# One core, cosine attention into a leaky-relu MLP: every operation issued from one written list

## The chip, the cores and the metric

One core of a Trainium2 chip runs the kernel. The metric is the time of one execution in device microseconds; the kernel before was timed three times, and its median is 416.56 us (415.56 to 416.66). Five engines work side by side, each through its own instructions in order: TensorE (PE; its weight loads are shown as PEld), VectorE (DVE), ScalarE (ACT), GpSimd (POOL) and SyncE (SP). SP and POOL also issue the DMAs, each in the order of its own queue; ACT issues three at the very start.

## The reference, cut

```python
def _attn_ref(q, k, v, tau):          # 8 x 12 x 448 x 64 each, tau = 0.1
    q_n = q / (np.linalg.norm(q, axis=-1, keepdims=True) + 1e-06)
    k_n = k / (np.linalg.norm(k, axis=-1, keepdims=True) + 1e-06)
    scores = np.matmul(q_n, k_n.transpose(0, 1, 3, 2)) / tau
    scores = scores - np.max(scores, axis=-1, keepdims=True)
    attn = np.exp(scores)
    attn = attn / (np.sum(attn, axis=-1, keepdims=True) + 1e-09)
    return np.matmul(attn, v)

def _moe_ref(x, w_in, w_out):         # 3584 x 768, 768 x 2048, 2048 x 768
    h = x @ w_in
    g = np.maximum(0.01 * h, h)
    return g @ w_out
```

The heads of a batch are put side by side between the two (x has 8 x 448 rows and 12 x 64 columns). All inputs and the output are float32; the kernel multiplies in bf16.

## The kernel before

**Slots.** The 96 heads are worked off as 48 slots of q and k, each some 448 KB. Slots 0 to 11 (batches 0 and 1) hold one pair of heads each, q and k together; slots 12 to 47 come in twos, q of two pairs of heads in the even one and k in the odd one, and two such slots are a *unit*. A slot passes through: load (`load_qk`, on SP; slots 0 to 5 are loaded ahead of everything), squares on POOL (L226, L218), sums of the squares on DVE (`sums`, L240, L234), square roots on ACT (`roots`: a logarithm and an exponential, L247 and L248), and `normalise` on DVE (reduce and reciprocal, L255 and L256, and the multiply that writes the bf16 tile qn, L272, L262). Slots 0 to 11 are then transposed on PE against an identity (L286) and copied out of PSUM by DVE (L327); the others are transposed on DVE (L308) and laid out as qkT by six DMAs of SP for each unit (L317).

**Attention.** A score tile is 128 keys by two heads of 448 queries and takes two banks of PSUM: `scores` for slots 0 to 11 (L348; three tiles for a slot, and a fourth for the keys that remain of two slots), `quad_tiles` (L419, seven tiles for a unit) after that. ACT takes the exponential of each into a bf16 tile pe (L357, L425). The sums over the keys and the products with v run on 32-column strips of PE (L368 for the first six j, a j being four heads; L444 for the ten groups of units). ACT turns the sums into reciprocals (L379 and L380, L453 and L456), and DVE multiplies the products by them into xT (L399, L469, L475), the transposed input of the MLP.

**MLP.** It goes by eight chunks c, one for a batch (384 or 512 columns). `first(c, m)` makes one of 16 tiles of the hidden layer: six matmuls with w_in (L496), then a leaky relu on ACT into hT (L507). `second(c, ts, half)` makes 128 rows by 384 columns of the output: 16 matmuls with w_out (L533), a copy by DVE (L543), and a store by SP (L550) when the row is whole. For chunk 0 the tiles of `first` can be done in parts, so many of the six matmuls at a time.

**Loads on POOL's queue.** v in pieces (`load_v`, L178, one for each of the first six j; `load_v_rem`, L186, what remains of them; `load_vq`, L204, one for each group), w_in in four parts of 768 KB (`load_w_in`, L104) and w_out in three: the first half of its columns whole (1536 KB), and the second half in two parts, rows 0 to 7 and 8 to 15 of its 16 blocks (`load_w_out`, L110).

**Holds.** Two helpers only make a queue wait. `hold` lets POOL copy one element of a slot's qn (L618), and what POOL issues after it waits until that slot is normalised. `hold_loads(s)` does the same to SP's queue with a DMA of one element of qn of slot s into the tile `behind` (L615).

**Banks.** `banks(count)` deals the eight banks of PSUM to the matmuls, always the ones dealt longest ago, unless one is kept. While `deals["apart"]` holds, that is in the loop over the first six slots, pairs come from banks 0 to 3 and single ones from 4 to 7.

**What sets the order.** Slots 0 to 5 run in a loop (L654 to L736), slots 6 to 11 in a stretch written out by hand (L747 to L863), and the rest in visits of three quad tiles each (L868 to L963), into which whole tiles of `first` and `second` are dealt by their cost. Between them stand *fills*: matmuls on constant data (L607), 20 at the start and then in threes and twos, 37 in all. In the loop the sums of a later slot stand around the norm of the next one:

```python
        if n and s > 1:
            sums(n, (0,))
        if not last:
            normalise(s + 1)
        ...
        elif s in (2, 3):
            hold_loads(s + 1)
            load_qk(s + 6)
```

and in the stretch by hand, with s = 6, stand `load_v(s // 2 + 1)`, `load_w_out(1, 0, MT // 2)`, later `load_w_out(1, MT // 2)`, `load_v(s // 2 + 2)`, and the holds and loads `hold_loads(s + 3)`, `load_qk(s + 6)`, `hold_loads(s + 4)`, `load_qk(s + 7)`, `hold_loads(s + 5)`, `load_qk(s + 8)`, `load_qk(s + 9)`.

**Buffers.** Four for loaded slots, three each for qn, squares and norms, six for qkT, 25 for pe, three for v of the first six j, two for v of the groups, one for hT, three for output rows.

Of the kernel before, what the change touches and what calls it, by code (L numbers as in the profile page):

```python
# [12 lines left out]
AX = mybir.AxisListType  # L13


@with_exitstack
def kernel(
# [25 lines left out]
    WARM = 20  # L43
    NEWQ = 2 * NQ
    PER = 3
# [25 lines left out]
    age = [0] * 8  # L71
    kept = {}
    deals = {"n": 0, "apart": True, "width": 128}

    def banks(count, keep=None):
        lo, hi = (0, 8) if not deals["apart"] else (0, 4) if count == 2 else (4, 8)
        x = min(
            (i for i in range(lo, hi, count) if not set(range(i, i + count)) & set(kept.values())),
            key=lambda i: max(age[i : i + count]),
        )  # L80
        deals["n"] += 1
        age[x : x + count] = [deals["n"]] * count
        if keep:
            kept[keep] = x
        return ps[:, x] if count == 1 else ps[:, x : x + count]

    def given_back(keep):
        deals["n"] += 1
        age[kept.pop(keep)] = deals["n"]

# [115 lines left out]
    def squares(s, eng=gp, parts=(0, 1)):  # L211
        if s >= NSLOT:
            return
        sq = sqt[s % 3]
        if s >= OLD:
            sqs[s] = sq
            x = raw[s].rearrange("p (t d) -> p t d", d=D)
            gp.tensor_tensor(sq[:, :, :D], x, x, op=ALU.mult)  # L218
            return
        sqs[s] = halves(sq.rearrange("p t d -> p (t d)"), D + 1)  # L220
        for i in parts:
            x, y = raw[s][i], sqs[s][i]
            if eng is nc.scalar:
                nc.scalar.activation(y[..., :D], x, func=AF.Square)
            else:
                eng.tensor_tensor(y[..., :D], x, x, op=ALU.mult)  # L226

    def sums(s, parts=(0, 1)):
        if s >= NSLOT:
            return  # L230
        if s not in ss:
            ss[s] = smp.tile([128, 14], F32, name="ss")
        if s >= OLD:
            nc.vector.tensor_reduce(  # L234
                ss[s], sqs[s], axis=AX.X, op=ALU.add
            )
            return
        for i in parts:
            o = ss[s][:, 0:8] if i == 0 else ss[s][:, 8:14]
            nc.vector.tensor_reduce(  # L240
                o.rearrange("p (h t) -> p h t", h=2), sqs[s][i], axis=AX.X, op=ALU.add
            )

    def roots(s):
        if s >= NSLOT:
            return
        nc.scalar.activation(ss[s], ss[s], func=AF.Ln)  # L247
        nc.scalar.activation(norms[s % 3][:, :, 0], ss[s], func=AF.Exp, scale=0.5)  # L248
# [3 lines left out]
    def normalise(s):  # L252
        if s >= NSLOT:
            return
# [29 lines left out]
    def one(tp, s, lo, hi):  # L284
# [10 lines left out]
    def transposed():  # L295
        return banks(1).bitcast(BF16)[:, : 7 * 128].rearrange("p (t c) -> p t c", c=128)
# [3 lines left out]
    def transposes(s):  # L300
        if s >= NSLOT:
            return
        if s >= OLD:
            u, which = divmod(s - OLD, 2)
            if which == 0:
                turned[u] = ttp.tile([128, 2, 2, S], BF16, name="tt")
            to = turned[u][:, :, which].bitcast(F32)
            nc.vector.transpose(  # L308
                out=to.rearrange(("p g (c m) -> p m g c", "p g (m c) -> p m g c")[which], m=7),
                in_=qn[s].bitcast(F32).rearrange("p m (g c) e -> p m g (c e)", g=2),  # L310
            )
            if which == 0:
                return
            for w, pair in enumerate(UNITS[u][1]):
                dst = qtp.tile([128, 2, S], BF16, name="qkT")
                for r0, of, n, g in ((0, 0, 32, 0), (32, 0, 64, 1), (96, 32, 32, 0)):
                    nc.sync.dma_start(  # L317
                        out=dst[r0 : r0 + n],
                        in_=turned[u][64 * w + of : 64 * w + of + n, g],
                    )  # L320
                qkT[pair] = dst.rearrange("p t c -> p (t c)")
            return
        dst = qtp.tile([128, 7, 128], BF16, name="qkT")
        qkT[s] = dst.rearrange("p t c -> p (t c)")
        tp = transposed()
        one(tp, s, 0, 7)
        nc.vector.tensor_copy(out=dst, in_=tp)  # L327
# [6 lines left out]
    def scores(s, kis):  # L334
        key_tiles([(s, ki) for ki in kis])

    def key_tiles(which):

        tiles = []
        for s, ki in which:  # L340
            sc = banks(2)
            tiles.append(sc)
            width = deals["width"] if ki < 3 else min(deals["width"], 64)
            for p in range(0, 128, width):
                x, c0 = (qkT[s - 1 + p // 64], 448 + p % 64) if ki == 3 else (qkT[s], 512 + 128 * ki + p)
                for a in range(2):
                    rows = slice(64 * a, 64 * a + 64)
                    nc.tensor.matmul(  # L348
                        out=sc[p : p + width, a, :S], lhsT=x[rows, c0 : c0 + width],
                        rhs=x[rows, 0:S], start=True, stop=True,  # L350
                    )
        for (s, ki), sc in zip(which, tiles):
            if ki == 3:
                dst = pr[s // 2] = pe_tile()
            else:
                dst = pe[s, ki] = pe_tile()
            nc.scalar.activation(out=dst, in_=sc[:, :, :S], func=AF.Exp, scale=inv_tau)  # L357
# [17 lines left out]
    def totals(j):  # L375
        sm = banks(1)
        strip_products(j, sm, lambda g, ki: ones, lambda g: ones_rem[:, g // 2])
        rb = rbp.tile([128, 2, S], F32, name="rb")[:, 0]
        nc.scalar.activation(rb, sm[:, :S], func=AF.Ln)  # L379
        nc.scalar.activation(rb, rb, func=AF.Exp, scale=-1.0)  # L380
        rbs[j] = rb

    pos = {}

    def products(j, e, po=None):
        b, jj = divmod(j, NQ)
        if po is None:
            po = banks(1, (j, e))
        pos[j, e] = po
        vm = vb[j].rearrange("p h t (d e) -> p h t e d", e=2)  # L390
        vr = vrb[b % 2].rearrange("p j g (d e) -> p j g e d", e=2)
        strip_products(j, po, lambda g, ki: vm[:, g, ki, e], lambda g: vr[:, jj, g, e])

    def scale(j, e):
        b, jj = divmod(j, NQ)
        m, half = divmod(b, 2)
        if m not in xT:
            xT[m] = xtp.tile([128, KT, 2 * S], BF16, name="xT")
        nc.vector.tensor_tensor(  # L399
            xT[m][:, 2 * jj + e, half * S : (half + 1) * S], pos.pop((j, e))[:, :S], rbs[j],  # L400
            op=ALU.mult,
        )
        if (j, e) in kept:
            given_back((j, e))
# [3 lines left out]
    def quad_tiles(which):  # L408

        tiles = []  # L410
        for u, i in which:
            sc = banks(2)
            tiles.append(sc)
            for strip in range(4):
                x = qkT[UNITS[u][1][strip // 2]]
                c0 = S + 64 * i + 32 * (strip % 2)
                for a in range(2):
                    rows = slice(64 * a, 64 * a + 64)
                    nc.tensor.matmul(  # L419
                        out=sc[32 * strip : 32 * strip + 32, a, :S], lhsT=x[rows, c0 : c0 + 32],  # L420
                        rhs=x[rows, 0:S], start=True, stop=True,
                    )
        for (u, i), sc in zip(which, tiles):
            pq[u, i] = pe_tile()
            nc.scalar.activation(out=pq[u, i], in_=sc[:, :, :S], func=AF.Exp, scale=inv_tau)  # L425
# [3 lines left out]
    def group_products(g, e):  # L429


        us = [u for u, (gg, _) in enumerate(UNITS) if gg == g]
        two = len(us) == 2
        po = banks(2)
# [14 lines left out]
        return po  # L449

    def group_logs(g, po):
        grb[g] = rbp.tile([128, 2, S], F32, name="rb")
        nc.scalar.activation(grb[g], po[:, :, :S], func=AF.Ln)  # L453
# [10 lines left out]
    def group_scale(g, e, po):  # L464
        js = GROUPS[g]
        for w in range(2):
# [6 lines left out]
            for n in range(2):  # L473
# [4 lines left out]
                )  # L478

# [7 lines left out]
    def first(c, m, kts=range(KT)):  # L487
        c0, n = chunk_cols(c)
        if c not in hT:
            hT[c] = htp.tile([128, MT, 512], BF16, name="hT")  # L490
        if (c, m) in begun:
            pm, done = begun.pop((c, m))
        else:
            pm, done = banks(1, (c, m, "begun") if len(kts) < KT else None), 0
# [7 lines left out]
        if done + len(kts) < KT:  # L502
            begun[c, m] = pm, done + len(kts)
            return
        if (c, m, "begun") in kept:
            given_back((c, m, "begun"))
        nc.scalar.activation(out=hT[c][:, m, :n], in_=pm[:, :n], func=AF.Prelu, alpha=0.01)  # L507

# [16 lines left out]
    def second(c, ts, half):  # L525
# [472 lines left out]
```

## Time and profile before

| what | value |
|---|---|
| median of three runs | 416.56 us |
| the profiled execution: its time, its span | 416.8 us, 415.0 us |
| PE from its last matmul to the end of the span | 2.9 us |
| score tile, exponential of it | 0.19 us of PE, 0.84 us of ACT |
| six w_in matmuls of 384, of 512 columns | 0.98 us, 1.30 us |
| 16 w_out matmuls | 2.60 us |
| square, sum, norm of a late slot | 1.69 (POOL), 1.05 and 1.6 us (DVE) |
| landing of a late slot's q, k | 4.1, 4.6 us after the issue |

The span runs from the first to the last instruction; the execution's own time is 1.8 us longer. In the profile a line number is that of the kernel before; "idle before" is how long the engine stood still ahead of a group, with what ended it. Landing is counted from the issue of a DMA to the arrival of its last byte.

### The profile page before, as it was taken

Reading aid. Unit: us, or ns where it says so; the run is one execution under the profiler, and the core shown is the slowest. Engines: PE = TensorE matmul, PEld = TensorE weight load, DVE = VectorE, ACT = ScalarE, POOL = GpSimd, SP = SyncE. Lnnn points to the kernel's source line nnn. Section 1 sums busy time; section 2 is a strip of 40 time slices with the busy share of each in tenths; the row PEclk is TensorE's granted clock in tenths of the full one; section 3 lists DMA queues with packets and bytes.
Section 4 is the critical chain, followed back from the end, with each engine's and each line's share of the span. In section 5 each row is a group of like instructions: output and inputs, shape, how many; then the busy total and the mean of one; then the engine's idle time right before and its main releaser. Section 6 shows DMA issues by size and latency. Waiting matters only on the chain.

```text
span 415.0 us, 11326 instructions
## 1 busy us (share of the span) xinstructions
PE 405.8 (98%) x4783; PEld 212.2 (51%) x4799; DVE 221.4 (53%) x387; ACT 250.5 (60%) x431; POOL 115.1 (28%) x150
## 2 busy tenths in 40 slices
PE   8799999999999999999999999999999999999997
PEld 3235555544555555544455555554445555654465
DVE  5878879756778556766484964464621301210021
ACT  4997877378657785667865688547764464004300
POOL 4885556133234132413331433122210000000000
PEclk9999999999999999999999999999999999999999
DMA  7999998965377851884285681742442100020022
GB/s 184 233 208 222 216 232 176 258 178 127 57 208 184 206 127 24 206 230 97 51 190 153 149 235 44 173 128 84 91 90 66 53 39 3 38 77 0 2 76 76
DMA packets 41980, 53.82 MB, mean 130 GB/s; under 512 B 12490, under 2 KB 32330, under 8 KB 41930
## 3 DMA queue, kind: packets, MB, share of 16 engines
q1 hardware_dynamic: 25738, 41.01, 35.1%
q0 software_dynamic: 15504, 11.80, 19.8%
q8 instruction: 37, 0.61, 0.6%
q10 hardware_dynamic: 688, 0.30, 0.2%
q14 instruction: 13, 0.11, 0.1%
HBM read 45.61 MB, written 11.01 MB: 136 GB/s over the span
## 4 chain that ended last, share of the span: by engine, by line
PE 93%; DMA 2%; ACT 1%; POOL 1%; SPq 1%; issue 1%; DVE 0%; POOLq 0%
PE ps L533 36%; PE ps L496 36%; PE ps L444 9%; PE ps L419 7%; PE ps L368 3%; PE ps L348 2%; DMA xT<-in_k_dram 1%; DMA xT<-in_q_dram 1%; ACT pe L357 1%; POOL sq L226 1%; PE ps L286 1%; SPq L133 0%; DVE qn L272 0%; POOL v_rem L186 0%; SPq L141 0%
## 5 line engine op out<-in xcount | busy, mean ns | idle before, releaser
L533 PE MATMUL ps<-w_out_sb,hT 128*128 128x384 bf16 (+1 forms) x912 | 151.3, 323 | 0.0
L496 PE MATMUL ps<-xT,w_in_sb 128*128 128x384 bf16 (+1 forms) x754 | 150.1, 352 | 0.8 <-issue 0.2
L425 ACT ACTIVATE pe<-ps 128x896 bf16<-128x896 f32 x126 | 108.9, 916 | 47.1 <-PE ps L419 47.1
L533 PEld LDWEIGHTS <-hT 128*128 128x128 bf16 x912 | 86.5, 98 | 64.0 <-issue 10.3
L496 PEld LDWEIGHTS <-w_in_sb 128*128 128x128 bf16 x768 | 72.6, 98 | 74.3 <-issue 9.8
L507 ACT ACTIVATE hT<-ps 128x384 bf16<-128x384 f32 (+1 forms) x128 | 67.4, 553 | 56.1 <-PE ps L496 54.9
L543 DVE COPY osb<-ps 128x384 f32<-128x384 f32 (+1 forms) x57 | 31.2, 547 | 101.4 <-PE ps L533 101.3
L218 POOL TENSOR_TENSOR sq<-qk_h 128x896 f32<-128x896 f32 x36 | 60.9, 1691 | 13.0 <-DMA qk_h<-in_k_dram 8.5
L618 POOL CAST seen<-qn 128x1 f32<-128x1 bf16 x46 | 8.5, 185 | 166.3 <-DVE qn L262 156.5
L262 DVE TENSOR_TENSOR qn<-qk_h,r 128x896 bf16<-128x896 f32 x36 | 43.3, 1203 | 1.2
L234 DVE TENSOR_REDUCE ss<-sq 128x14 f32<-128x910 f32 x36 | 37.9, 1053 | 1.1 <-POOL sq L218 1.1
L357 ACT ACTIVATE pe<-ps 128x896 bf16<-128x896 f32 x42 | 36.0, 918 | 2.4 <-PE ps L348 2.3
L419 PE MATMUL ps<-qkT 64*32 64x448 bf16 x1008 | 36.5, 353 | 0.0
L255 DVE TENSOR_REDUCE r<-norms 128x14 f32<-128x28 f32 x48 | 8.6, 178 | 48.7 <-ACT norms L248 48.1
L469 DVE TENSOR_TENSOR xT<-ps,rb 128x448 bf16<-128x448 f32 x32 | 18.4, 615 | 23.2 <-PE ps L444 21.5
L308 DVE STREAM_TRANSPOSE tt<-qn 128x448 f32<-128x448 f32 x36 | 29.6, 821 | 0.9
L444 PE MATMUL ps<-pe,vq 64*32 64x448 bf16 x1008 | 27.0, 349 | 0.0
L247 ACT ACTIVATE ss<-ss 128x14 f32<-128x14 f32 x48 | 10.3, 215 | 23.6 <-DVE ss L234 23.1
L419 PEld LDWEIGHTS <-qkT 64*32 64x32 bf16 x1008 | 13.0, 91 | 19.2 <-issue 14.2
L444 PEld LDWEIGHTS <-vq 64*32 64x32 bf16 x1008 | 14.5, 92 | 8.0 <-issue 0.3
L444 PE MATMUL ps<-pe,ones 64*32 64x448 bf16 x560 | 15.1, 349 | 0.0
L348 PE MATMUL ps<-qkT 64*64 64x448 bf16 (+1 forms) x132 | 12.8, 359 | 2.1 <-ACT pe L357 1.2
(53 smaller groups left out, 218.1 us busy)
## 6 DMA issues: line engine op xcount, KB each, us to landing
qk_h<-in_q_dram SPq DMA_DIRECT2D x36, 224.0 KB, 4.1
qk_h<-in_k_dram SPq DMA_DIRECT2D x36, 224.0 KB, 4.6
out_dram<-osb SPq DMA_DIRECT2D x20, 384.0 KB, 2.3
qkT<-tt SPq DMA_DIRECT2D x72, 56.0 KB, 3.2
qkT<-tt SPq DMA_DIRECT2D x36, 112.0 KB, 3.4
vq<-in_v_dram POOLq DMA_DIRECT2D x16, 224.0 KB, 4.7
w_in_sb<-in_moe_w_in_dram POOLq DMA_DIRECT2D x4, 768.0 KB, 10.4
out_dram<-osb SPq DMA_DIRECT2D x15, 192.0 KB, 3.7
```

The costliest lines, as they stand in the source:

```text
L218: gp.tensor_tensor(sq[:, :, :D], x, x, op=ALU.mult)
L234: nc.vector.tensor_reduce(ss[s], sqs[s], axis=AX.X, op=ALU.add)
L262: nc.vector.tensor_tensor(qn[s].rearrange("p m d e -> p m e d"), raw[s].rearrange(f"p ({t[1:-1]} d) -> p m e d", e=n, d=D), r.rearrange(f" ...
L308: nc.vector.transpose(out=to.rearrange(("p g (c m) -> p m g c", "p g (m c) -> p m g c")[which], m=7), in_=qn[s].bitcast(F32).rearrange("p ...
L357: nc.scalar.activation(out=dst, in_=sc[:, :, :S], func=AF.Exp, scale=inv_tau)
L419: nc.tensor.matmul(out=sc[32 * strip : 32 * strip + 32, a, :S], lhsT=x[rows, c0 : c0 + 32], rhs=x[rows, 0:S], start=True, stop=True,)
L425: nc.scalar.activation(out=pq[u, i], in_=sc[:, :, :S], func=AF.Exp, scale=inv_tau)
L444: nc.tensor.matmul(out=po[32 * strip : 32 * strip + 32, w, :S], lhsT=weights, rhs=pq[us[x if two else 0], i][rows, a, :], start=(i == 0), ...
L496: nc.tensor.matmul(out=pm[:, :n], lhsT=w_in_sb[:, kt, m * 128 : (m + 1) * 128], rhs=xT[c // 2][:, kt, c0 : c0 + n], start=(done + i == 0), ...
L507: nc.scalar.activation(out=hT[c][:, m, :n], in_=pm[:, :n], func=AF.Prelu, alpha=0.01)
L533: nc.tensor.matmul(out=po2[:, : hi - lo], lhsT=hT[c][:, m, ts * 128 : (ts + 1) * 128], rhs=w_out_sb[:, m, half * HALF + lo : half * HALF + ...
L543: nc.vector.tensor_copy(out=o[:, cols], in_=po2[:, : hi - lo])
```

## The change

All operations are now issued by one loop over a written list, `ORDER`. Each entry is a name and its numbers, looked up in a table of functions. What belonged together in one helper is taken apart, so that each engine's part has an entry of its own: a matmul group and what reads it from PSUM are two steps (`k` and `x`, `q` and `y`, `f` and `r`, `s` and `o`). Banks are taken by the matmul's step under its name and given back by the reader's step; the one dealt is the one given back longest ago. The entry `tg` ends the time in which pairs and single banks come from apart halves; it stands ahead of the first score tile.

The names that the text uses: `lq` load a slot, `sq su ro no` its squares, sums, roots and norm (for slots below 12 in two parts, `.0` and `.1`), `tp tc` transposes and their copy, `tt td` transpose on DVE and the six layout DMAs, `k x` score tile and exponential of slots 0 to 11, `q y` the same for a unit, `to ln in` totals and their reciprocals of a j, `pr sc` product and scaling, `g gl gi gx` the same of a group, `f r` a tile of `first` (with the matmuls meant, if not all six) and its relu, `s o` a tile of `second` and its copy and store, `lv lr lg wi wo` the loads on POOL, `hp` and `hs` the holds of POOL and SP, `w` fills. So `f.0.3.0.1.2.3` is chunk 0, tile 3, matmuls 0 to 3.

```diff
+ORDER = """
+lq.6 qf.0.0.3 qf.1.0.3 uf.0.0.3 w.20 qf.0.3.4 sq.2.0 uf.1.0.3 sq.2.1 uf.0.3.4 lr.0.2.4 w.2 ro.0 no.0 sa.1.0
+sa.1.1 tp.0.4.7 tp.0.0.4 w.3 w.2 ta.0.0.4 su.1.1 su.1.0 tc.0.4.7 lr.0.0.2 su.2.1 ro.1 no.1 hr k.0.1 sq.3.1 tg
+lv.0 k.0.0 su.2.0 w.2 w.2 x.0.1 k.0.2 tp.1 x.0.0 x.0.2 sq.3.0 tc.1 k.1.2 ro.2 k.1.0 lq.7 k.1.1 su.3.1 x.1.2
+no.2 w.2 x.1.0 w.2 k.1.3 tp.2 su.3.0 tc.2 w.2 w.2 x.1.1 k.2.1 sq.4.1 wi.0 hp.1 hp.0 k.2.0 ro.3 x.1.3 no.3
+x.2.1 x.2.0 to.0 ln.0 sq.4.0 hp.2 lv.1 sq.5.1 k.2.2 tp.3 su.4.0 su.4.1 tc.3 k.3.2 k.3.1 pr.0.0 ro.4 sq.5.0
+x.2.2 su.5.1 wi.1 in.0 k.3.0 hp.3 x.3.2 x.3.0 sq.6.1 lv.2 sq.7.0 sq.6.0 no.4 tp.4 su.5.0 sc.0.0 tc.4 k.3.3
...
+lq.8 sc.1.0 su.6.0 wi.2 x.4.1 k.5.0 k.5.1 x.5.1 wi.3 sq.7.1 pr.1.1 sc.1.1 sq.8.0 f.0.1.0.2 k.5.3 k.5.2 x.5.0
+x.5.2 x.5.3 ro.6 f.0.3.0.1.2.3 f.0.0.0.2 f.0.0.1 sq.8.1 wo.0 hs.3 lq.9 f.0.1.3 f.0.2.0.1.2.3 su.8.0 to.2 ln.2
...
+f.0.13 ro.9 x.7.0 no.8 f.0.10 f.0.11 x.7.3 tp.8 lq.11 sq.10.1 no.9 k.6.1 k.7.2 r.0.10 tc.8 f.0.7 sq.11.0
+wo.1.0.8 hp.8 sq.11.1 x.7.2 r.0.13 x.6.1 f.0.8 tp.9 f.0.12 su.10.0 su.10.1 r.0.7 r.0.11 tc.9 f.0.14 r.0.8
+ro.10 r.0.12 k.8.2 r.0.14 x.8.2 no.10 su.11.0 k.8.1 k.8.0 to.3 tp.10 f.0.15 tc.10 su.11.1 x.8.0 x.8.1 ln.3
+r.0.15 f.0.9 k.9.1 k.9.0 ro.11 lq.13 hs.10 lq.12 hs.9 no.11 in.3 r.0.9 k.9.2 x.9.2 s.0.0.0.384 x.9.1 x.9.0
+tp.11 hs.11 o.0.0.0.384 pr.3.0 sq.12 lv.4 wo.1.8 pr.3.1 tc.11 k.10.0 sc.3.0 sc.3.1 su.12 k.10.1 k.9.3 hp.10
+sq.13 lq.15 su.13 s.0.1.0.384 x.10.1 sq.15 x.9.3 ro.12 x.10.0 no.12 k.11.0 k.11.1 k.11.2 x.11.0 tt.12 x.11.2
+s.0.2.0.384 k.10.2 lq.14 ro.13 x.11.1 x.10.2 k.11.3 x.11.3 pr.4.1 no.13 o.0.1.0.384 tt.13 su.15 to.4 to.5 lv.5
+hp.12 hp.13 hp.11 sq.14 pr.4.0 td.0 lq.17 ln.5 ln.4 in.5 ro.15 in.4 no.15 sc.4.0 o.0.2.0.384 su.14
...
+y.1.2 r.1.9 gl.0 r.1.14 r.1.15 q.1.5 q.1.6 no.20 hp.16 hp.18 g.0.0 no.19 lq.21 lq.23 r.1.13 y.1.5 q.2.0 hp.20
+sq.23 s.1.0.0.384 lq.22 gi.0 y.1.6 s.1.1.0.384 y.2.0 q.2.1 gx.0.0 o.1.0.0.384 tt.19 su.23 sq.21 hp.19 q.2.3
+sq.22 su.22 su.21 q.2.2 y.2.2 o.1.1.0.384 tt.20 y.2.1 ro.23 y.2.3 ro.21 s.1.0.384.768 lq.25 td.3 o.1.0.384.768
+q.2.6 q.2.5 q.2.4 s.1.2.0.384 s.1.1.384.768 y.2.4 y.2.5 ro.22 y.2.6 q.3.1 q.3.0 no.23 no.21 lq.24 o.1.2.0.384
...
+"""
...
-    def banks(count, keep=None):
+    age, taken = [0] * 8, {}
+    deals = {"n": 0, "apart": True}
+
+    def take(name, count):
         lo, hi = (0, 8) if not deals["apart"] else (0, 4) if count == 2 else (4, 8)
+        busy = {b for x, n in taken.values() for b in range(x, x + n)}
         x = min(
-            (i for i in range(lo, hi, count) if not set(range(i, i + count)) & set(kept.values())),
+            (i for i in range(lo, hi, count) if not busy & set(range(i, i + count))),
             key=lambda i: max(age[i : i + count]),
         )
+        taken[name] = x, count
+        return ps[:, x] if count == 1 else ps[:, x : x + count]
...
+    def give(name):
+        x, count = taken.pop(name)
         deals["n"] += 1
         age[x : x + count] = [deals["n"]] * count
...
+    for step in ORDER.split():
+        name, *args = step.split(".")
+        steps[name](*map(int, args))
```

## The prediction

> **What bounds the kernel now.** First the page's busy shares and its 40 slices.
>
> ```profile
> span 415.0 us, 11326 instructions
> ...
> PE 405.8 (98%) x4783; PEld 212.2 (51%) x4799; DVE 221.4 (53%) x387; ACT 250.5 (60%) x431; POOL 115.1 (28%) x150
> ...
> PE   8799999999999999999999999999999999999997
> ...
> DMA  7999998965377851884285681742442100020022
> ```
>
> PE is the bound: 9.2 us idle in all. Of these the windows by stage put about 5.4 us before 32 us (1.7 us until the first fill, then gaps of 0.2 to 1.4), 0.8 us between 80 and 390, and 2.9 us after the last matmul. So an order can win little, and it loses whatever PE waits. The DMA row is full up to slice 7 (72 us); that matters below. The chain of waits, asked for 12 to 34 us, shows the one large gap of the head:
>
> ```profile
> 17.59 1.00 POOL sq L226
> ...
> 18.62 0.03 DVE ss L240
> ...
> 19.23 0.18 DVE r L255
> ...
> 19.71 1.17 DVE qn L272 x2
> ...
> 20.92 0.34 PE ps L286 x3
> ```
>
> The fourth norm (`no.3`, L255) stands behind a fifth sum (`su.4.0`, L240), which waits for POOL's square; PE sat idle 1.35 us before the transposes. From about 33 us PE is never short of work. Next the queues behind the loads: the timelines of SP and POOL between 45 and 70 us, and from the DMA view the landings.
>
> ```profile
> 49.23 0.63 SPq L615 DMA_DIRECT2D behind<-qn  x1
> 49.96 1.14 SPq L152 DMA_DIRECT2D qk_h<-in_q_dram  x2
> 54.51 0.60 SPq L615 DMA_DIRECT2D behind<-qn  x1
> 55.20 1.11 SPq L152 DMA_DIRECT2D qk_h<-in_k_dram  x2
> 59.09 0.60 SPq L615 DMA_DIRECT2D behind<-qn  x1
> ```
>
> ```profile
> 48.13 0.82 POOL L178 DMA_DIRECT2D v_b<-in_v_dram  x1
> 48.95 0.90 POOL L110 DMA_DIRECT2D w_out_sb<-in_moe_w_out_dram  x1
> ...
> 54.60 0.94 POOL L110 DMA_DIRECT2D w_out_sb<-in_moe_w_out_dram  x1
> 55.55 0.76 POOL L178 DMA_DIRECT2D v_b<-in_v_dram  x1
> ...
> 57.90 1.68 POOL L218 TENSOR_TENSOR sq<-qk_h 128x896 f32<-128x896 f32 x1
> ```
>
> ```profile
> w_out_sb<-in_moe_w_out_dram POOLq DMA_DIRECT2D x2, 768.0 KB, 14.6
> ...
> v_b<-in_v_dram POOLq DMA_DIRECT2D x6, 192.0 KB, 9.2
> ```
>
> The three `behind` DMAs are `hs.9`, `hs.10`, `hs.11`. Slot 10's norm ends at 52.56 (timeline of DVE), yet `hs.10` goes out at 54.51, 5.28 us after `hs.9`; `hs.11` follows 4.58 us later, `hs.4` in the head 4.88 us after `hs.3`. All write one element of one tile; I read it so that each waits until the one before has landed: holds in a row cost about 4.9 us each. `lv.4` goes out at 48.13 and lands at 57.2 (9.1 us); the second part of the second half of w_out (`wo.1.8`) goes out at 54.60 and lands at 69.7; PE reads it from 72.1 on. Landings on POOL's queue come in order of issue: `lv.3`, issued 3.6 us after `wo.0`, took 19.9 us and landed 1.0 us after it.
>
> **The change, part by part.** Counted name by name, old driver and list hold the same 1,250 steps, the same parts of `first` and the same 37 fills; only order and deal of banks differ. Work added: 0 on every engine. I lay the durations of the rows end to end along both lists, with PE without a gap from `to.2` (33.4 us) on, and ask at each step how late what it needs would be.
>
> *Switches of PE.* Three tiles of L419 after 128-row work take 0.69 us, two after a product 0.38, so entering costs 0.69 - 3 x 0.19 = 0.12; 16 matmuls of L533 take 2.71 after strips, 2.60 after L496, so leaving costs 0.11. From `to.2` on, the old order goes in 53 times, the new one 52; from `q.0.0` on both 43 times. Worth **-0.2 us**.
>
> *The head.* Two more fills (2 x 0.215) stand before the first transposes, so the first exp (10.37) comes about 0.5 us later. `no.3` no longer waits for the fifth sum and comes about 1.3 us sooner. Between 10.4 and 33.7 us ACT idles about 2 us in all, so its 21 exps and what lies between set the pace; summed along the new list the last (`x.5.3`) ends 0.2 us sooner. Before `to.2` PE now does 14 w_in matmuls instead of 8: 6 x 0.163 = 1.0 us. Together **-1.2 us**. Bounds: -3.5 (every gap but the first closed) to +0.9: `wi.1` goes out behind both squares of slot 5, some 1.5 us later than 20.12, and lands after 10.0 us at 31.6 or later, where the third part of `first` wants it at 31.4. `lq.8`, now ahead of `hs.3`, adds 448 KB to that stretch, but takes it from the next.
>
> *Banks up to 55 us.* With all eight dealt, `k.7.0`, `k.7.2`, `f.0.7` take banks whose reader (a relu or exp) ends 0.5 us late by the sums: **+0.5** (0 to 0.8).
>
> *SP between 45 and 65 us.* Old: `hs.9 lq.12 hs.10 lq.13 hs.11 lq.14 lq.15`. New: `lq.13 hs.10 lq.12 hs.9 hs.11 lq.15 lq.14`. `lq.13` wins 9 us; `lq.12` now stands behind the hold of slot 10. Norm of 10 ends at about 52.4, `hs.10` 52.4, `lq.12` 53.1, its second DMA 53.8; landing 6.4 us (this load before), so 60.2 (4.1, its kind's median, to 7.2: 57.9 to 61.0). `hs.9` then waits until 57.3, `hs.11` until 62.2: `lq.15` goes out at 62.9 instead of 61.1, `lq.14` at 64.2 instead of 59.8.
>
> *POOL.* Old: `lv.4 wo.1.0.8 hp.10 sq.11 wo.1.8 lv.5 hp.11 sq.12`. New: `sq.11.0 wo.1.0.8 hp.8 sq.11.1 sq.12 lv.4 wo.1.8 hp.10 sq.13 sq.15 lv.5`. So `lv.4`, `wo.1.8` and `lv.5` now queue behind squares that wait for loads. `sq.12` 60.2 to 61.9, `lv.4` out at 61.9; landing between 6.0 (fastest v_b row) and 9.1: 67.9 to 71.0; with `sq.12` at its earliest 65.6, with the slowest near row, 15.3 us, 77.2. I take 69.5, as `wo.1.0.8` ahead of it (out about 50.4, 14.1 us) is through by 64.5. PE wants it for `pr.4.1`, now in front of `to.4`: from `to.2` 82 w_in matmuls (13.3), 3 x 16 of L533 (7.8), 21 score tiles (3.9), six groups of transposes (2.3), six of strips (4.5) and switches (2.0), end at 67.2, with the 0.5 above 67.7. In the old order it lands 11.5 us before its product starts (68.72); that cover is gone: **+1.8 us** (0 to +9.5). Behind it on PE stand both totals, and `wo.1.8` is next: out at 62.7, 10.4 us (w_in's four of the same size: 7.7 to 12.0; its own row 15.1), 73.1; PE gets to row 8 of it at 69.5 + 3.1 + 1.3 = 73.9. `lv.5`, behind `sq.15`, out at 71.5, lands at 77.5 to 80.6; wanted at 77.9. Together **+0.5** (0 to +4).
>
> *From 80 us on.* Loads, turns and visits are shuffled by up to 22 places, and room is given up: between 90 and 125 the sums bring readers 0.5 to 1.6 us late at some fifteen places, where the old order has none. The worst: `lq.23` out at 106.1 lands at 110.8; `sq.23 sq.21 hp.19 sq.22` (3 x 1.69 + 0.19) until 116.1; `su.22 su.21` until 118.2; only then DVE copies `o.1.1.0` out of the bank that PE wants for `s.1.2.0` at 116.4. A PE that is already 2 us late hides part. **+1.0** (0 to +3). The other lates, up to 1.1 near 207, lie within that slip. The shuffled tiles of `first` and their relus cost nothing while a relu (0.46 to 0.6) fits under the next tile (1.0 to 1.3); from 240 us on nothing is late by over 0.15. The tail is as before: last piece, copy, 96 KB store.
>
> Sum: -0.2 - 1.2 + 0.5 + 1.8 + 0.5 + 1.0 = +2.4 on the span of 415.0: 417.4. Around it lie 1.8 us (run of 416.8), and that run is 0.24 above the median of 416.56: **419.0 us**.
>
> **Rivals.** That the list is not what it says is none: `no.3` does stand ahead of `su.4.0`, and all eight banks are dealt from before `k.0.1` on. *A, faster: the loads come in time.* The place is `pr.4.1` at 67.2, the price lv.4's landing; it decides if that is before about 67.5. For it: with `lv.4`, `wo.1.8` and `lq.13` gone from 53 to 60 us, the queues hold only `wo.1.0.8` and `lq.12`, so 4.1 and 6.0 us may be the right rows. Against it: no v_b row before 60 us but two is under 9. Then -0.2 - 1.2, and the tight places cost 0.3 or win as much: 416.56 - 1.4 to -2.0, about **414.8**. *B, even.* `lv.4` costs 1, the rest 0.5: **416.6**. *C, the order is tight throughout.* If loads take 5.2 us and turns 6.9 (q and k, and tt, in the busier stretches) instead of 4.4 and 5.9, the lates between 90 and 170 grow to 3 or 4 us, and with `lv.4` at 71.0 the slip is 5 to 6: **421.5**. For it: by the sums 10 steps of PE find something more than 0.2 us late in the old order, 33 in the new. *D, PE falls to half rate.* The first fills run at 0.43 us each, the later ones at 0.215, although the granted clock is shown as 1.00; a wait of 3.5 us at `pr.4.1` might bring that back, 13 fills' time (5.6 us) at half rate, +2.8: **424**. The Trainium skill, "TensorE: Matmul & The Clock Gate", Part 1, says that PE's clock halves after an idle window of some 3.4 us and returns after as much work. No run here has such a gap; by that rule D follows from any wait that long, by the granted clock of the trace it would not.
>
> **How the numbers follow.** Forecast 0.38, A 0.27, B 0.15, C 0.13, D 0.07. A measurement of this kernel tells 0.3% (1.25 us) from no change. Slower: 0.38 + 0.13 + 0.07 = 0.58; same 0.15; faster 0.27. The forecast's own range is 417.9 to 420.8. For 8 in 10 the range goes down to 414.0 (most of A) and up to 422.5 (C, not D).
>
> **What would show it.** Right: on SP three `behind` DMAs with 4.5 to 5 us between, `lq.15` and `lq.14` after 62; `lv.4` issued after 59 behind L218; PE idle 1 us or more before the first product of j = 4, named as waiting for v_b. The gap at 19 us gone, `to.2` at 33.4 with 14 w_in matmuls before it. Wrong: no PE gap between 60 and 80 us (A), or gaps elsewhere that sum to more (C). The head is wrong if PE waits for w_in at 31 us. The forecast falls if PE's busy time changes by more than 1 us, since the work is the same.

## The result, and the profile after

The changed kernel takes **429.52 us** (median of six runs, 426.16 to 431.55), the kernel before 416.51 us beside it: a ratio of 1.0304, 95% interval 1.0257 to 1.0352. The forecast was 419.0 us: slower, as foreseen, but by 13 us instead of 2.5. The profiled execution took 429.4 us, its span is 427.4 us. In every ratio here an execution counts only if it is within 1.5% of the fastest of its kernel, which leaves out one each of e2, e7 and e13 below. Line numbers are now those of the kernel that ran: in the experiments the same line stands up to six lines higher, as the list has another length.

The page after, its first lines:

```profile
span 427.4 us, 11306 instructions
...
PE 407.8 (95%) x4782; PEld 213.8 (50%) x4799; DVE 225.4 (53%) x387; ACT 245.4 (57%) x431; POOL 122.0 (29%) x150
```

PE's work is the same, yet it now covers 95% of the span. Of the 12.4 us that the span grew, 10 are idle time of PE ahead of its last matmul (16.3 us now, 6.3 before), 2.0 are busy time, and 0.4 are the tail (3.3 us behind the last matmul, 2.9 before). The view of PE's waits names the idle time (who waits, for whom, us in total, times, longest):

```profile
PE ps L374 <- DVE qn L359: 2.7, 4, 0.9
PE ps L427 <- DVE qkT L390: 2.1, 3, 1.1
PE ps L568 <- ACT hT L582: 2.1, 2, 1.7
...
PE ps L492 <- ACT hT L582: 1.2, 1, 1.2
...
PE ps L450 <- DMA v_b<-in_v_dram: 0.2, 1, 0.2
```

The first two lines are the head (up to 29 us). The wait for v_b on which the forecast put most is 0.2 us. The relus (hT) that PE waits for are ACT's, 3.3 us of them, and exps take another 2.9; ACT is 57% busy, so it is not slow, it stands behind something. Three places show behind what.

**The head.** The chain of waits, 9 to 29 us, runs over DVE almost alone; two of its five norms (L359, two instructions each; start and time in us):

```profile
14.77 2.32 DVE qn L359 x2
...
18.77 1.16 DVE qn L359 x2
```

Before, most norms of this shape took 1.2 us. The fourth (18.77) is no longer waited for; those of slots 1, 2, 4 and 5 now take 0.5 to 1.0 us longer than they did (slot 1 1.72 at 11.05, slot 4 2.08 at 22.40, slot 5 2.16 at 26.54). POOL's timeline has what runs beside that of slot 2:

```profile
14.38 2.29 POOL L306 TENSOR_TENSOR sq<-xT 128x512 f32<-128x512 f32 x2
...
17.43 0.44 POOL L677 CAST seen<-qn 128x1 f32<-128x1 bf16 x2
```

Two squares, which take 2.29 us here and 1.82 where no norm runs, and only behind them the holds (`seen`, L677) of slots 1 and 0, which before stood ahead of the squares. Beside the norm of slot 1 POOL squares nothing; it issues four loads of v (9.97 to 12.63 us). What lengthened that norm is not shown: in the kernel before, the one at 19.71 kept its 1.16 us beside two loads. `to.2` starts at 34.56 us, 1.19 later than before; 1.0 of that are the six more w_in matmuls that now stand ahead of it, so by this trace the head lost 0.2 us. Other executions of the same head lost more (e5 and e9, below).

**80 to 98 us.** Timelines of SP, POOL, ACT and PE (start, us, instruction, in brackets the idle time before it and what ended it):

```profile
80.32 1.35 SPq L628 DMA_DIRECT2D out_dram<-osb  x2
81.78 4.67 SPq L230 DMA_DIRECT2D qk_h<-in_q_dram  x6
...
89.78 3.32 POOL L300 TENSOR_TENSOR sq<-qk_h 128x896 f32<-128x896 f32 x2 [13.94 <-DMA qk_h<-in_q_dram]
...
94.27 0.21 ACT L336 ACTIVATE ss<-ss 128x14 f32<-128x14 f32 x1 [7.01 <-DVE ss L316]
...
94.64 0.58 ACT L582 ACTIVATE hT<-ps 128x512 bf16<-128x512 f32 x1
...
95.27 1.46 PE L568 MATMUL ps<-xT,w_in_sb 128*128 128x512 bf16 x6 [1.74 <-ACT hT L582]
```

Read it upward: PE waits 1.74 us for a relu; the relu stands on ACT behind a root (L336), which has waited 7.01 us for its sum; the square on POOL has waited 13.94 us for a load. It is slot 16's: on SP it stands behind that of slot 20, and both behind the store of a finished row that waits for PE and DVE (80.32). Before, it went out at 74.31, ahead of the stores.

**217 us.** The same chain again (load, square, sum, root, relu), and then something more. Windows of 3.4 us (busy time of PE, weight loads, DVE, ACT and POOL with counts, granted clock of PE, DMA):

```profile
216.90:220.30 3.40, 1.78 (x37) 0.71 (x21) 2.46 (x5) 3.37 (x8) 3.34 (x6) 1.00 0.63 95
220.30:223.70 3.40, 3.40 (x12) 1.63 (x11) 0.00 (x0) 0.92 (x2) 0.47 (x2) 0.50 0.92 211
```

PE idles 1.62 us of one window, and in the next its clock is 0.50: 3.41 us of work at half speed, 1.7 us lost, which is nearly all of the 2.0 us of added busy time. The six runs sort by it, roughly: the one at a mean clock of 1.00 took 426.2 us, those at 0.996 (one such window) 426.6 and 429.4, those at 0.992 (two) 429.7 to 431.6.

### The profile page after: what moved, and what is told of

Its sections match the earlier page's. It is cut to its first block, busy times and chain, and to the rows that moved or that the text cites. A ratio compares the mean times of both kernels' runs of the same rounds, so it can differ in the third digit from the quotient of the medians.

```text
span 427.4 us, 11306 instructions
## 1 busy us (share of the span) xinstructions
PE 407.8 (95%) x4782; PEld 213.8 (50%) x4799; DVE 225.4 (53%) x387; ACT 245.4 (57%) x431; POOL 122.0 (29%) x150
## 4 chain that ended last, share of the span: by engine, by line
PE 68%; DVE 13%; DMA 7%; POOL 3%; SPq 3%; issue 3%; ACT 2%; DVEq 0%; POOLq 0%; ACTq 0%
PE ps L604 27%; PE ps L568 27%; PE ps L518 8%; PE ps L492 5%; DMA qk_h<-in_q_dram 4%; DVE qn L359 3%; POOL sq L300 3%; DVE ss L316 2%; DVE ss L319 1%; DVE qn L349 1%; SPq L230 1%; DMA qk_h<-in_k_dram 1%; DVE xT L550 1%; PE ps L450 1%; DVE tt L400 1%
## 5 line engine op out<-in xcount | busy, mean ns | idle before, releaser
L604 PE MATMUL ps<-w_out_sb,hT 128*128 128x384 bf16 (+1 forms) x912 | 153.3, 326 | 1.1 <-DVE osb L620 0.6
L568 PEld LDWEIGHTS <-w_in_sb 128*128 128x128 bf16 x768 | 73.4, 98 | 77.9 <-issue 12.7
L300 POOL TENSOR_TENSOR sq<-qk_h 128x896 f32<-128x896 f32 x36 | 62.3, 1737 | 140.5 <-DMA qk_h<-in_q_dram 74.1
L582 ACT ACTIVATE hT<-ps 128x384 bf16<-128x384 f32 (+1 forms) x128 | 64.0, 548 | 66.1 <-PE ps L568 35.1
L620 DVE COPY osb<-ps 128x384 f32<-128x384 f32 (+1 forms) x57 | 29.9, 543 | 99.1 <-PE ps L604 96.9
L349 DVE TENSOR_TENSOR qn<-qk_h,r 128x896 bf16<-128x896 f32 x36 | 47.8, 1328 | 2.8 <-DVE r L343 0.9
L400 DVE STREAM_TRANSPOSE tt<-qn 128x448 f32<-128x448 f32 x36 | 28.6, 810 | 6.0 <-DMA qkT<-tt 5.8
L336 ACT ACTIVATE ss<-ss 128x14 f32<-128x14 f32 x48 | 10.3, 216 | 30.9 <-DVE ss L316 28.3
L677 POOL CAST seen<-qn 128x1 f32<-128x1 bf16 x46 | 12.5, 273 | 24.9 <-DVE qn L349 20.1
L282 POOL DMA_DIRECT2D vq<-in_v_dram x20 | 12.6, 635 | 13.5 <-PE ps L518 12.7
```

Of the source, the lines that this page charges most:

```text
L349: nc.vector.tensor_tensor(qn[s].rearrange("p m d e -> p m e d"), raw[s].rearrange(f"p ({t[1:-1]} d) -> p m e d", e=n, d=D), r.rearrange(f" ...
L400: nc.vector.transpose(out=to.rearrange(("p g (c m) -> p m g c", "p g (m c) -> p m g c")[which], m=7), in_=qn[s].bitcast(F32).rearrange("p ...
L568: nc.tensor.matmul(out=pm[:, :n], lhsT=w_in_sb[:, kt, m * 128 : (m + 1) * 128], rhs=xT[c // 2][:, kt, c0 : c0 + n], start=(done + i == 0), ...
L604: nc.tensor.matmul(out=po2[:, : hi - lo], lhsT=hT[c][:, m, ts * 128 : (ts + 1) * 128], rhs=w_out_sb[:, m, lo:hi], start=(m == 0), stop=(m ...
L620: nc.vector.tensor_copy(out=o[:, lo:hi], in_=bank(("s", c, ts, lo))[:, : hi - lo])
```

## The experiments

Each is the changed kernel, or the old order issued from the list, with one stretch or queue altered; "old order" is that of each engine in the kernel before. One thing goes along with it in some runs. Banks are dealt by the order of the whole list, and where the engines' sequences were joined to a new list, the deal is another one, though PE's order is kept: against the changed kernel, 334 of 413 deals are other in e6, e7 and e14, the same 334 in all three, and 292 in e10; against e1, 214 in e8 and 108 in e12. In e4, e5, e9, e13 and e15 the deal is the changed kernel's; e2, e3 and e11, which join two orders, have deals of their own. e8 and e12 also have five loads of SP ahead of a store, as the kernel before does, where e1 has them behind it. What the runs with another deal are worth holds this too. "Over before" is the ratio less one, times 416.5 us, against the kernel before on the same chip (the changed kernel: 12.7 us).

| run | altered | ratio to before, 95% | over before |
|---|---|---|---|
| e1 | old order from the list | 1.0010 [0.9996, 1.0024] | 0.4 |
| e2 | new, old head | 1.0064 [1.0041, 1.0088] | 2.7 |
| e3 | old, new head | 1.0114 [1.0062, 1.0165] | 4.7 |
| e4 | new, slot 16 loaded first | 1.0246 [1.0210, 1.0282] | 10.2 |
| e5 | new, w_in sooner | 1.0293 [1.0268, 1.0319] | 12.2 |
| e6 | new, POOL and DVE old in the head | 1.0220 [1.0205, 1.0235] | 9.2 |
| e7 | new, queues old at 45 to 70 us | 1.0221 [1.0154, 1.0288] | 9.2 |
| e8 | e1, norm 3 ahead | 1.0026 [1.0017, 1.0036] | 1.1 |
| e9 | new, late slots in turn | 1.0133 [1.0108, 1.0159] | 5.5 |
| e10 | e6, e7 and e9 together | 1.0086 [1.0070, 1.0102] | 3.6 |
| e11 | old to 104 us, then new | 1.0166 [1.0151, 1.0182] | 6.9 |
| e12 | e1, holds behind squares | 1.0056 [1.0038, 1.0073] | 2.3 |
| e13 | new, square of slot 35 later | 1.0320 [1.0234, 1.0405] | 13.3 |
| e14 | e6 and e7 together | 1.0170 [1.0152, 1.0188] | 7.1 |
| e15 | new, loads of 36 and 37 exchanged | 1.0210 [1.0187, 1.0232] | 8.7 |
| e16 | before, norm 3 ahead | 0.9997 [0.9987, 1.0007] | -0.1 |

### Which stretch: e1 to e4 and e11

e1 issues every engine's old sequence from a list, by which the banks are dealt; e2 and e3 join one order up to `to.2` to the other one after it. In these three a few stores of finished rows stand at other places among SP's loads than in the order they come from; in e2 that puts the loads of slots 20 and 16 ahead of one store, so it holds part of e4 as well.

> Every engine and both queues in the order of the kernel before, issued from the list, banks given back by the readers and dealt from all eight from the first score tile on. Theory Q (the loss is in the order of loads and squares on the queues) and theory V (it is in the order of visits on PE and ACT) both: 416.0 to 417.5 us, PE idle 9 to 10 us. If the dealing of banks or the list itself costs: over 418.5.

> Old order up to the totals of j = 2 on every engine, new order after it. Theory H (the head lost because squares run over norms): to.2 back at 33.4 with 8 matmuls of first before it, so 0.3 us won against the changed kernel by the trace, 428.5 to 429.5 us, and the norms of slots 1 to 5 back at 1.2 to 1.3 us each (now 1.7 to 2.3). If the head were the cause of more (a late load that is felt later): 427 or less.

> New order up to the totals of j = 2, old order after it. If the loss lies behind the head (Q and V): 416.5 to 418. If what the head leaves late is felt later: over 419.

e1 is within 0.4 us of before: the list, and the banks that it deals, cost nothing that matters; the loss comes with the new order and the deal that follows from it. e2 and e3 both came out on the second side of what was expected: what the head leaves late is felt later. It is worth 4.7 us on the old rest, and the changed kernel with the old head loses 2.7 instead of 12.7. So behind an old head the late order, which e2 keeps but for slots 20 and 16 and some stores, costs 2.7 us at most; the prices below are those of one place in one kernel, not sums to be added. In e3 the one run at full clock took 418.1 us, the three with half-rate windows 422.1 to 423.1; a window costs 1.7 us, so two of them lost more than the clock explains, and they have no trace.

e4 moves two loads:

```diff
-td.0 lq.17 ... o.0.1.384.768 ... lq.20 lq.16 ... lq.18
+td.0 lq.17 lq.16 ... o.0.1.384.768 ... lq.18 lq.20
```

> The changed kernel with only the load of slot 16 moved ahead of the three copies and stores of chunk 0, and that of slot 20 behind that of slot 18. Theory Q: slot 16 issued at about 75 instead of 84.6, its square 7 us or more sooner, the PE gaps of 1.7 and 0.3 at 93 to 97 us gone and some of what follows with them: 425 to 427.5 us. Theory V: the relus stay late, gaps at 93 to 97 stay over 1.5 us, 429 to 430.

The load went out at 80.1 us, not 75 (SP was still at slot 17's), but that was enough. PE's timeline in e4:

```profile
85.41 12.91 PE L563 MATMUL ps<-xT,w_in_sb 128*128 128x512 bf16 x57
```

57 matmuls of `first` without a gap, where the changed kernel has two; 2.5 us won for two entries of 1,250, within what theory Q said, at its weak end. The gap is settled by the trace, the 2.5 us less so, as the two intervals overlap.

e11 asks the other way round: old order up to `g.0`, new after it.

> Old order on every engine up to the sums of group 0 (about 104 us), new order after it. By the gaps after 104 us in the changed kernel (0.7 at 123, 1.4 at 153, 1.6 at 217, small ones 0.5): 419.5 to 421.5. If these are only echoes of what came before: 417 to 418.5.

It lost 6.9 us, more than both answers. In its trace PE has no gap between 110 and 180 us, so those at 123 and 153 come from what stands ahead of 104 us (or from the deal of banks, which is another one here too); 1.1 us stand at the seam (103 us), and 2.2 at 212 to 233, so the one at 217 does not. Of the 6.9 us 3.3 are idle time of PE ahead of its last matmul, 0.4 the tail, and 3.2 busy time at full clock (409.0 us, 405.8 before). About 1 us of that is no work: the trace of before lacks 16 matmul records, and e16, the same work with all of them, has 406.8. No run explains the rest.

### The head: e5, e6, e12

```diff
 e5
-lv.1 sq.5.1 ... sq.5.0 ... wi.1
+lv.1 wi.1 sq.5.1 ... sq.5.0
-lq.8 ... hs.3 lq.9
+hs.3 lq.8 ... lq.9
 e6, POOL up to to.2 (DVE old there too)
-sq.2.0 sq.2.1 lr.0.2.4 lr.0.0.2 hr sq.3.1 lv.0 sq.3.0 sq.4.1 wi.0 hp.1 hp.0 sq.4.0 hp.2
+hr lr.0.0.2 hp.0 sq.2.0 sq.2.1 lv.0 hp.1 sq.3.0 sq.3.1 lr.0.2.4 wi.0 hp.2 sq.4.0 sq.4.1
 e12, on e1, POOL
-hp.0 sq.2.0 sq.2.1 lv.0 hp.1 sq.3.0 sq.3.1 ... hp.2 sq.4.0 sq.4.1
+sq.2.0 sq.2.1 hp.0 lv.0 sq.3.0 sq.3.1 hp.1 ... sq.4.0 sq.4.1 hp.2
```

> The changed kernel with the second part of w_in (wi.1) issued ahead of both squares of slot 5, as before, and the hold of slot 3 ahead of the load of slot 8 again. Theory W (the head's loss is late w_in and v, which share their time with a load too many, and the clock windows at half rate that such waits bring): wi.1 issued at about 20.3 instead of 22.0, landing by 31, no wait of PE for w_in or v_b before 40 us, 1 to 3 us won: 426.5 to 428.5. Theory N (the head's loss is squares that run over norms): 429 to 430.

> The changed kernel with POOL and DVE in the old order up to the totals of j = 2 (holds between the squares, so that fewer squares run while DVE normalises); PE, ACT and SP as changed. Theory N: the norms of slots 1, 2, 4 and 5 back from 1.7 to 2.3 us to 1.2 to 1.3, to.2 1.5 us or more sooner: 425 to 428 us. Theory W: wi.1 comes sooner in this order too, so a win alone does not tell N from W; a win over e5 of 1 us or more does.

> The old order (as e1) with POOL's holds of slots 0 to 5 each placed behind the squares of two slots later instead of ahead of them, nothing else. Theory N: squares now run while DVE normalises, norms of slots 1 to 5 at 1.5 to 2.3 us instead of 1.25, 1 to 3 us lost: 418 to 420. If the holds do nothing for the norms: 416.5 to 417.5.

e5 won 0.5 us, inside the two intervals: w_in alone is not what costs. e6 won 3.5, which is 3.0 over e5 (with another deal of banks, which e5 has not). Two of the norms in DVE's timeline of e6, those of slots 2 and 4:

```profile
14.23 1.24 DVE L353 TENSOR_TENSOR qn<-xT,r 128x512 bf16<-128x512 f32 x2
...
22.38 1.16 DVE L353 TENSOR_TENSOR qn<-xT,r 128x512 bf16<-128x512 f32 x2
```

e12 is the converse, on the old order: the holds step back behind the squares, the norms of slots 3 to 5 grow from 1.16 to between 1.69 and 2.17 us (those of slots 1 and 2 don't grow), PE's wait ahead of the transposes of slot 3 goes from 1.75 to 2.15 us, and 1.9 us are lost against e1. Not all of that is the holds': 0.69 us are a wait of PE for an exp at 220 us, which e8 has too and e1, with its other deal of banks, has not; and at `to.2` the two traces are only 0.3 us apart. That a hold of POOL, at 0.2 us, keeps the next square off the norm holds from both sides; its price is less sure, up to 3.5 us by e6 and about 1 by e12.

The traced execution of the changed kernel was a lucky one in this stretch. e9, further below, has the same head to the last entry, and in its trace the norms of slots 1 and 3 are

```profile
11.41 2.97 DVE L354 TENSOR_TENSOR qn<-xT,r 128x512 bf16<-128x512 f32 x2
...
19.45 3.04 DVE L354 TENSOR_TENSOR qn<-xT,r 128x512 bf16<-128x512 f32 x2
```

and `to.2` starts at 39.06 us (37.73 in e5). In the changed kernel and in e3, e4, e7, e13 and e15, which share its head, it starts at 34.6 to 35.5, and in e6, e10 and e14, where the holds stand as before, at 33.0 to 35.0. So, counted as above, the head lost 0.2 us in one execution and 4.7 in another; how often, the traces can't say.

### Which queue at 45 to 70 us: e7

```diff
-SP: lq.13 hs.10 lq.12 hs.9 hs.11 lq.15 lq.14
+SP: hs.9 lq.12 hs.10 lq.13 hs.11 lq.14 lq.15
-POOL: sq.11.0 wo.1.0.8 hp.8 sq.11.1 sq.12 lv.4 wo.1.8 hp.10 sq.13 sq.15 lv.5
+POOL: lv.4 wo.1.0.8 hp.8 hp.10 sq.11.0 sq.11.1 wo.1.8 lv.5 sq.12 sq.13 sq.15
```

> The changed kernel with the holds and loads of slots 12 to 15 on SP, and lv.4, both parts of w_out's second half and lv.5 on POOL, in the old order (lv.4 ahead of the squares of slot 12); all else as changed. By the prediction's terms 1.8 + 0.5: lv.4 out at about 48 to 50, no wait of PE between 60 and 80 us, 2.3 us won, 427. If those waits are hidden by what comes later (loads of slots 16 on): 429 to 430.

`lv.4` goes out at 48.00, PE has no wait between 60 and 80 us, and 3.5 us are won, with a wide interval: two of four runs have half-rate windows. At full clock its spans are 421.4 and 422.0 us, the changed kernel's is 424.1: 2.1 to 2.7 us, near the 2.3 of the prediction. By the traces 0.4 of it comes between 34 and 54 us, where PE's wait of 0.8 us for a bank at 48.8 is gone with the other deal.

### The late slots: e9, e13, e15

e9 keeps the places of all loads, squares, sums, roots, norms, holds and turns of slots 16 to 47, but deals the slots to them in the order of their numbers:

```diff
-lq.17 ... lq.20 lq.16 ... lq.18 ... lq.19
+lq.16 ... lq.17 lq.18 ... lq.19 ... lq.20
-sq.20 ... sq.19 ... sq.23 sq.21 ... sq.22
+sq.19 ... sq.20 ... sq.21 sq.22 ... sq.23
...
```

> The changed kernel with the loads, squares, sums, roots, norms, holds and turns of slots 16 to 47 in the order of their numbers, each at the places where the list has such a step (124 entries differ); head, spot at 45 to 70 and the order of PE's work as changed. Theory S (a later slot ahead of an earlier one makes the earlier one late, and its sums and roots hold up relus, exps and copies): the PE gaps at 93 to 97 (2.1 us), 123 (0.7), 153 (1.4) and 217 (1.6) shrink to under 1.5 us in all, 423 to 425.5. Theory V (the order of visits on PE): gaps stay or move, 428 to 430.

This is the largest single piece, 7.2 us. Of PE's six kinds of waits in e9 (the two left out are the start's 1.7 us and 0.4 us for a copy at 54 us):

```profile
PE ps L369 <- DVE qn L354: 5.7, 6, 1.6
PE ps L422 <- DVE qkT L385: 2.1, 2, 1.3
...
PE ps L513 <- DMA vq<-in_v_dram: 0.4, 1, 0.4
...
PE ps L563 <- DVE osb L615: 0.2, 1, 0.2
```

Not one for a relu or an exp is left, though the order of PE's and ACT's work is the new one: theory S, not V. After 55 us 0.6 us of waiting are left, and that in an execution whose head was worse than the changed kernel's (four norms of 2.6 to 3.6 us). e9 has the changed kernel's deal of banks, so this price is that of the slots' order alone.

e13 and e15 ask whether one overtaking slot is enough for the gap at 217 us.

```diff
 e13, POOL
-sq.32 sq.35 hp.30 sq.33 hp.31 hp.29 sq.34
+sq.32 hp.30 sq.33 hp.31 hp.29 sq.35 sq.34
 e15, SP
-lq.37 lq.36
+lq.36 lq.37
```

> The changed kernel with one entry moved: the square of slot 35 behind the square of slot 33 and the holds 31 and 29, ahead of that of slot 34. Theory S: POOL no longer waits for the load of slot 35 before it squares slot 33, whose roots stand ahead of relus on ACT; the PE gaps of 1.2 and 0.4 us at 217 to 220 us go, and the half-rate window after them: 426 to 428 us. Theory V: gap stays, 429 to 430.

> The changed kernel with the loads of slots 36 and 37 exchanged, nothing else. In e13's trace it was slot 36's load, not slot 35's square, that was late: it goes out 1.2 us behind that of slot 37. Theory S: slot 36 squared 1.2 us sooner, the PE wait for a relu at 217 us down from 1.2 to 1.6 to under 0.4: 427.5 to 428.5 us, 1 to 3 under 429.5 as no half-rate window follows. If the turn ahead of both loads sets the time: wait of 1 us or more as before, 429 to 431.

e13 missed: the gap stayed at 1.35 us. The slot had been read wrongly from the list. Its timeline of SP has a load of k, then one of q, and POOL waiting for the q: slots 37 and 36. e15 exchanges those two. Its view of PE's waits has, where the changed kernel has 1.2:

```profile
PE ps L487 <- ACT hT L577: 0.2, 1, 0.2
```

No half-rate window follows in this execution, and 4.0 us are won, more than theory S gave. The gap had been just long enough to halve the clock; the two together, 1.0 and 1.7 us by the traces, make 2.7, and the rest stays open.

### Do they add up: e10, e14

> e9 with the old head on POOL and DVE (as e6) and the old order of SP and POOL at 45 to 70 us (as e7): only the order of PE's and ACT's work and the bank deals are the new ones from there on. If the three account for the loss: 416.5 to 418.5. Theory V: 421 or more.

> e6 and e7 together: old order of POOL and DVE in the head, old order of SP and POOL at 45 to 70 us, slots from 16 on in the changed kernel's order. If the terms add up: 429.5 - 4.3 - 3.2 = 422.0. If PE, being earlier, waits longer for the late slots behind it (as the win of the old order with the fourth norm ahead was given back): 424 to 425.5, with larger gaps at 93 to 97 and at 217 us.

Singly the three are worth 3.5, 3.5 and 7.2 us, together 9.1 (e10); the first two together 5.6 (e14, 423.76 us: less than their sum, but not for the reason given, as PE's gap at 93 us is down to 0.3). They overlap, so "account for the loss" was wrong in size: 3.6 us over before stay with the three undone. Part of the overlap may be the deal of banks that e6, e7 and e14 have in common, which then counts twice; no run changes it alone. The 3.6 us aren't split here. In e10's trace 0.9 us of them are a wait for vq and 0.8 the tail (3.7 us); the new order of PE's, ACT's and DVE's own work and the places of its steps between loads are candidates that no run isolates.

### Is the fourth norm worth anything: e8, e16

```diff
-        if n and s > 1:
+        if n and s > 2:
             sums(n, (0,))
         if not last:
             normalise(s + 1)
+        if s == 2:
+            sums(n, (0,))
```

(e16; e8 is the same on e1, `su.4.0 no.3` to `no.3 su.4.0` on DVE.)

> The old order from the list (as e1) with the norm of slot 3 ahead of the first sum of slot 4 on DVE, and nothing else. By the prediction's reading of the head the gap of 1.4 to 1.8 us ahead of the transposes of slot 3 shrinks to under 0.5 us: 415.5 us, 1.0 to 1.4 under e1 (416.9). If ACT's exps or w_in set the pace of the head: 416.5 to 417.

> The kernel before, with its own driver and bank deals, and only the first sum of slot 4 moved behind the norm of slot 3. If the head sets the time of what follows: the gap of 1.35 us at 19 us down to under 0.7, 415.2 to 415.8. If what comes after the head (landings of w_in and v, holds) sets it, as e8 says: 416.2 to 417.

In both the gap at 19 us shrinks as foreseen (in e16 from 1.35 us to nothing, its transposes 2.0 us sooner than in the trace of before), and in both nothing that can be measured comes of it: e16 is level with before within 0.1%, e8 0.7 us behind e1. e8 shows where such a lead can go. It is 2.2 us ahead of e1 at 33 us (e1's trace has a half-rate window at 22 us, which is part of that), 0.7 at 62, and level at 220; its view of PE's waits:

```profile
PE ps L445 <- DMA v_b<-in_v_dram: 0.5, 1, 0.5
PE ps L563 <- DMA w_in_sb<-in_moe_w_in_dram: 0.4, 1, 0.4
```

PE comes sooner to w_in (30.6 us) and to v (32.7) and waits for them there. The last 0.7 us go at 219 us, where it waits for an exp; that is not the lead's doing, as e12, which is late and not early, has the same wait. No version run here beats the kernel before.

## Why the prediction was right or wrong

- **The bound** was read rightly: PE is short of nothing but work that others bring late. *Switches*, -0.2: no run isolates them.
- **The head, -1.2**: wrong. The gap at 19 us went, but `to.2` came at 34.56 with its 14 w_in matmuls, not at 33.4, and in e9 at 39.06. The step that failed: norms and squares were laid end to end at their old durations, POOL beside DVE, and a hold was priced at its 0.2 us. What the holds kept apart had no price. The runs showed norms of 1.7 to 3.6 us in place of 1.2, worth 3.5 us by e6 and about 1 by e12, both with a change in the deal of banks; the head as a whole is worth 4.7 on the old rest (e3) and 10.0 on the new (e2). That w_in could be late was inside the bounds; e4, with the same head, shows 0.9 us of that wait, the changed kernel's trace none.
- **Banks, +0.5**: e1 gives 0.4 [-0.2, 1.0] for the list and its banks together, but 325 of its 413 deals are not those of the changed kernel, so the term has no test of its own. The one wait that looks like it is 0.8 us at 48.8 us, for a DVE copy; it is 0.4 to 0.8 in the runs with the same deal and gone in e6, e7, e10 and e14. (In the list `tg` stands behind the first score tile, not ahead of it: all eight banks are dealt one tile later than was said.)
- **SP and POOL at 45 to 70 us, +1.8 and +0.5**: right about the queues and, nearly, in size, wrong about the path to PE. The timelines of SP, POOL, ACT and PE:

```profile
57.97 5.13 SPq L674 DMA_DIRECT2D behind<-qn  x2
...
64.83 0.83 POOL L256 DMA_DIRECT2D v_b<-in_v_dram  x1
...
66.06 0.21 ACT L336 ACTIVATE ss<-ss 128x14 f32<-128x14 f32 x1 [1.36 <-DVE ss L316]
...
67.38 0.38 PE L427 MATMUL ps<-qkT 64*64 64x448 bf16 x4 [1.06 <-ACT pe L438]
```

`lq.15` and `lq.14` go out at 63.20 and 64.45, forecast for 62.9 and 64.2; `lv.4` at 64.83 behind the square of slot 12, forecast for 61.9, as that slot's load went out at 54.92, not 53.1, and took 7.6 us where 6.4 were put. PE's wait was named wrongly: 1.06 us of it fall on a bank whose exp is late, 0.18 on v. The exp stands on ACT behind the root of slot 12 (66.06), which waits for that slot's sum, and so for the same late load: it is the chain of 80 us, one stretch sooner, and the prediction put no price on it.
- **From 80 us on, +1.0**: the largest error, 7.2 us by e9. The lates had been found, 0.5 to 1.6 us at some fifteen places; what failed is the step that followed, "a PE that is already 2 us late hides part". Lateness hid nothing: in e7 and e14 (both with another deal of banks) PE comes to `g.0` about 3 us sooner, and the gaps at 93, 123 and 153 us add up to 0.8 us instead of 4.1. A load can stand behind a store that PE and DVE release, as at 80 us, and is then late with PE; that this is so at every gap is not shown. And a late slot does its harm through ACT, where its root stands in front of relus that had all they needed (94.27 us): with the slots in turn no such wait is left.
- **The tail**, taken as unchanged, is 0.4 us longer.
- **The rivals.** C ("tight throughout", 421.5) was the kind of thing that happened, at less than half its price. D had the right effect under too strict a condition: the clock did halve, but after waits of 1.6 us, not 3.5. That PE's busy time grew by over 1 us, named as what would overturn the forecast, is this window. A fell by its own condition (`lv.4` landed at 71.1, not before 67.5), and B with it.

## What to carry to other kernels

An instruction that only makes a queue wait may be the cheapest in the program: before moving one, ask which two engines it keeps apart, and price that, not its own 0.2 us. Where several streams are in flight, keep them in turn on every queue: a stream ahead of its turn delays the one that is needed first, and the delay shows up three engines further, as a wait for an engine that is half idle. And a gain in one stretch is kept only if the next stretch is not waiting for something else (e8), while losses were passed on. Last, where buffers are dealt by the order of a list, moving an entry may deal them otherwise as well: a run that is to test the one has to keep the other.

## What the runs showed of the hardware

**Norms and squares exclude each other.** Timelines of POOL and DVE in the changed kernel:

```profile
143.57 2.54 POOL L300 TENSOR_TENSOR sq<-qk_h 128x896 f32<-128x896 f32 x1 [8.78 <-DVE r L343]
...
148.26 1.69 POOL L300 TENSOR_TENSOR sq<-qk_h 128x896 f32<-128x896 f32 x1
...
143.45 1.16 DVE L349 TENSOR_TENSOR qn<-qk_h,r 128x896 bf16<-128x896 f32 x1
...
147.72 3.27 DVE L349 TENSOR_TENSOR qn<-qk_h,r 128x896 bf16<-128x896 f32 x1
```

The norm at 143.45 began first and kept its 1.16 us; the square that began 0.12 us later took 2.54 instead of 1.69. At 147.72 POOL was issuing a load of v (146.88 to 148.12): the norm began during that, and the square of 148.26 went ahead of it as well; it ended 1.04 us after that square did. So the one that got in first held the other off until it was done. The Trainium skill, "SBUF — State Buffer", section "SBUF: two separate sides", says so: DVE with two operands in SBUF and GpSimd share a pair of ports under a lock that is held for the whole instruction. The trace agrees, and adds that a POOL that goes straight on can pass a waiting norm. Late in the kernel it costs nothing (from 60 us on e9 keeps four lengthened norms, up to 4.04 us, with no wait of PE behind them); in the head DVE is the chain.

**Half a window is enough to halve PE's clock.** In the profiled runs (e2's is left out) nine stretches of 3.41 us at half clock lie within the work; each follows a window of 3.41 us in which PE idled 1.62 to 2.53 us. No window with 1.56 us or less was followed by one, and three with 1.65, 1.71 and 1.95 us weren't either. The Trainium skill, "TensorE: Matmul & The Clock Gate", Part 1, has a free-running window of this length and speaks of an idle one; here the idle half of one did it. Several shorter waits can reach that together (1.19 and 0.43 us in the changed kernel's window at 217 us).
